# Loading the first scale group in two blocks on the ScalarE queue between exponentials, with c on the sync queue and a new k stage order

## The chip, the cores and the metric

The kernel runs on one core of a Trainium2 chip. The metric is the device time in microseconds (us) of one execution. The span of a profiled execution, from its first to its last instruction, is about 2 us shorter than the device time of the same execution (95.7 us of span for 97.58 us).

## The reference

It is the attention half of a diffusion transformer block with adaptive layer norm, in bfloat16, for B = 2, N = 256, D = 1152.

```
mod = silu(c) @ w_mod                      # c is B x D, w_mod is D x 6D
shift, scale, gate = three slices of mod
h = layernorm(x) * (1 + scale) + shift     # x is B x N x D
q, k, v = split(h @ wqkv)
a = (softmax(q @ k.T * D**-0.5) @ v) @ wo
return x + gate * a
```

## The kernel before

Tokens are four tiles of 128 (t = 0 to 3), features are nine slices of 128 (k = 0 to 8). A tile of x is normalised by VectorE, transposed by TensorE, multiplied by (1 + scale), and taken as the right operand of the k projection, feature slice by feature slice (`k_step(k, ...)`, weights `wK[k]`). The scale of a slice needs silu(c) and the matching part of the scale weights: nine small matmuls per slice. Those weights come in four groups, of 2, 2, 2 and 3 slices. The projection therefore can't start before x0 (tile 0 of x) is normalised and the first scale group has landed.

```python
load_x(syn, 0)                                    # sync queue
sca.dma_start(out=c_sb, in_=...)                  # c: ScalarE queue
S_GROUPS = SCALE_GROUPS                           # ((0, 2), (2, 4), (4, 6), (6, 9))
def load_scale(gi): ... syn.dma_start(out=wS_all[:, cols], in_=src)
...
junk(2)                                           # dummy 128x512 matmuls
ten.transpose(cT_ps, c_sb, ...)
sca.activation(out=e_sb, in_=cT_ps, func=ACT.Exp, scale=-1.0)
sca.activation(out=e_sb, in_=e_sb, func=ACT.Ln, bias=1.0)
sca.activation(out=e_sb, in_=e_sb, func=ACT.Exp, scale=-1.0)
...
junk(10)
stat_chunk(0, 1); stat_chunk(0, 0)
load_x(syn, 1); stat_sum(1); load_x(syn, 2)
...                                               # cut
norm(0, 0, 2); transposes(0, 0)
load_scale(0); scale_mods(0, 0, 9)                # first group: 576 KB, 18 small matmuls
...                                               # cut
load_wK(0); transposes(0, 1); load_wK(1)
k_step(0, 0, P); transposes(1, 0); ...; k_step(1, 0, P)
load_x(syn, 3); ...
load_scale(1); scale_mods(1, 0, 9)
...
```

Loads and their users are on different engines, so a load is issued as early as its own queue allows: the first scale group, behind the first transposes in the program, was issued at 2.11 us, before x0 had landed (3.61). On the sync queue the order is x0, x1, x2, first scale group, wK0, wK1, x3, second scale group, wK2, third scale group, and so on. Every load counts up one of eight completion semaphores, which are taken again in turn: the issue of a load waits until an earlier load on the same semaphore has landed. In the trace of this kernel the landings count on eight semaphores; the fourth scale group was issued at 8.40 us, after wK0 had landed at 8.39, and the load of wK behind it at 9.15, after wK1 had landed at 9.13.

## Time and profile before

| | before |
|---|---|
| device time, median (4 runs) | 98.44 us (98.36 to 98.59) |
| span of the profiled execution | 95.7 us |
| c landed | 2.85 us |
| x0, x1, x2 landed | 3.61, 4.36, 5.60 us |
| first scale group: issued, landed, first used | 2.11, 7.65, 7.91 us |
| wK0, wK1, second scale group landed | 8.39, 9.13, 11.32 us |
| first k step of slice 2 (`k_step(2, ...)`) starts | 12.72 us |

A landing here is the last increment of the load's completion semaphore in the trace, read to about 0.01 us; all times count from the start of the span.

The chain of waits, followed back from the last instruction (start us, us, what):

```profile
by line: PE ps L70 67.4%; PE acc_t L70 19.3%; PE psS L70 2.7%; DMA c_sb<-in_c_dram 2.2%; PE psH L70 2.2%; PE tp_t L70 1.7%; ACT o_sb L70 0.3%; DVE hTs L70 0.3%; PE cT_ps L70 0.2%; DVE s1p L70 0.2%; issue 0.2%; ACT L104 0.0%
...
0.75 2.10 DMA c_sb<-in_c_dram
...
3.52 4.38 PE acc_t L70 x10
...
8.11 0.49 PE psS L70 x18
...
12.38 0.30 DVE hTs L70
12.68 0.04 issue
12.72 1.14 PE acc_t L70 x9
```

In such lines PE is TensorE, DVE VectorE and ACT ScalarE; SPq and ACTq are issues on the sync and the ScalarE queue. psS is the result of the scale matmuls, tp_t of the transposes, acc_t of the dummies and the k steps; xn is a normalised tile, hTs a scaled one.

TensorE is the bound: after the load of c it runs nearly without a gap to the end. The ten dummies (3.52 to 7.9) keep it busy while the loads arrive. The waits of TensorE (in total, times, longest us) say the same: two, both before 3 us.

```profile
PE acc_t L70 <- DVE ones_w L70: 1.4, 1, 1.4
PE cT_ps L70 <- DMA c_sb<-in_c_dram: 0.4, 1, 0.4
```

### The profile page before, as it was taken

Reading aid. Unit: us, or ns where it says so; the run is one execution under the profiler, and the core shown is the slowest. Engines: PE = TensorE matmul, PEld = TensorE weight load, DVE = VectorE, ACT = ScalarE, POOL = GpSimd, SP = SyncE. Lnnn points to the kernel's source line nnn. Section 1 sums busy time; section 2 is a strip of 40 time slices with the busy share of each in tenths; the row PEclk is TensorE's granted clock in tenths of the full one; section 3 lists DMA queues with packets and bytes.
Section 4 is the critical chain, followed back from the end, with each engine's and each line's share of the span. In section 5 each row is a group of like instructions: output and inputs, shape, how many; then the busy total and the mean of one; then the engine's idle time right before and its main releaser. Section 6 shows DMA issues by size and latency. Waiting matters only on the chain.

```text
span 95.7 us, 1886 instructions
## 1 busy us (share of the span) xinstructions
PE 91.0 (95%) x771; PEld 60.9 (64%) x771; DVE 64.1 (67%) x131; ACT 32.3 (34%) x75; POOL 15.7 (16%) x11
## 2 busy tenths in 40 slices
PE   3899999999999999999999999999999999999980
PEld 0237989988899644444458765565568766556570
DVE  2487887050552999999999939910009599998780
ACT  5496988020421900003950084342335400000010
POOL 3020000000000000000000000079999900010000
PEclk9999999999999999999999999999999999999999
DMA  1999999999999999999993001122000000303122
GB/s 23 366 337 414 402 397 398 400 420 403 416 416 419 414 413 419 422 422 416 419 400 159 0 0 55 45 65 54 8 0 0 0 0 0 123 7 123 75 100 72
DMA packets 7379, 21.59 MB, mean 225 GB/s; under 512 B 2123, under 2 KB 2891, under 8 KB 7371
## 3 DMA queue, kind: packets, MB, share of 16 engines
q1 hardware_dynamic: 7200, 21.42, 57.7%
q8 instruction: 6, 0.10, 0.4%
q10 hardware_dynamic: 171, 0.05, 0.2%
q14 instruction: 2, 0.02, 0.0%
HBM read 19.76 MB, written 1.44 MB: 221 GB/s over the span
## 4 chain that ended last, share of the span: by engine, by line
PE 93%; DMA 2%; DVE 0%; ACT 0%; issue 0%
PE ps L70 67%; PE acc_t L70 19%; PE psS L70 3%; DMA c_sb<-in_c_dram 2%; PE psH L70 2%; PE tp_t L70 2%; ACT o_sb L70 0%; DVE hTs L70 0%; PE cT_ps L70 0%; DVE s1p L70 0%; ACT L104 0%
## 5 line engine op out<-in xcount | busy, mean ns | idle before, releaser
L70 POOL PARTITION_ALL_REDUCE gate_bc<-gacc x2 | 13.7, 6887 | 56.8 <-DVE gacc L70 56.8
L70 DVE SCALAR_TENSOR_TENSOR gacc<-wg_all,scT_f,gacc 128x1152 f32<-128x1152 bf16 x16 | 22.4, 1416 | 0.4
L70 PE MATMUL ps<-wV,hT 128*128 128x384 bf16 x108 | 17.7, 326 | 0.0
L70 PE MATMUL ps<-hT,wQ 128*128 128x512 bf16 x81 | 17.7, 379 | 0.0
L70 PEld LDWEIGHTS <-wK 128*128 128x128 bf16 x180 | 16.1, 98 | 1.8 <-issue 0.2
L70 PE MATMUL ps<-rows_t,attnT 128*128 128x384 bf16 (+3 forms) x108 | 17.0, 319 | 0.0
L70 PEld LDWEIGHTS <-attnT 128*128 128x128 bf16 x117 | 11.2, 98 | 6.4
L70 PEld LDWEIGHTS <-hT 128*128 128x128 bf16 x108 | 10.6, 98 | 6.9
L70 PE MATMUL acc_t<-hTs,wK 128*128 128x256 bf16 (+1 forms) x144 | 14.8, 259 | 0.1
L70 PEld LDWEIGHTS <-wQ 128*128 128x128 bf16 x81 | 7.9, 98 | 9.4
L70 ACT CAST v_sb<-ps 128x384 bf16<-128x384 f32 x12 | 5.8, 481 | 13.9 <-PE ps L70 13.9
L70 DVE CAST attnT<-ps 128x512 bf16<-128x512 f32 (+1 forms) x6 | 3.5, 603 | 9.5 <-PE ps L70 9.5
L70 ACT CAST qkT<-ps 128x512 bf16<-128x512 f32 x11 | 5.6, 610 | 12.6 <-PE ps L70 12.6
L70 DVE TENSOR_TENSOR ga<-ps,gate_bc 128x384 f32<-128x384 f32 (+3 forms) x12 | 6.4, 537 | 1.1 <-PE ps L70 1.0
L70 PE MATMUL acc_t<-ones_w 128*128 128x512 bf16 x12 | 5.5, 630 | 1.4 <-DVE ones_w L70 1.4
L70 DVE TENSOR_TENSOR o_sb<-ga,x_sb 128x384 bf16<-128x384 f32 (+3 forms) x12 | 6.5, 542 | 0.4
L70 ACT CAST o_sb<-ps 128x192 bf16<-128x192 f32 x1 | 0.3, 319 | 17.3 <-PE ps L70 17.3
L70 DVE CAST qkT<-acc_t 128x512 bf16<-128x512 f32 (+1 forms) x5 | 2.5, 576 | 4.5 <-PE acc_t L70 4.5
L70 DVE BATCH_NORM_STATS2 st_t<-x_sb 128x6 f32<-128x384 bf16 x6 | 3.1, 550 | 2.5 <-DMA x_sb<-in_x_dram 2.5
L70 PE MATMUL ps<-hTs,wK 128*128 128x256 bf16 x36 | 4.3, 272 | 0.0
L70 ACT ACTIVATE hTs<-xnT,s1p 128x128 bf16<-128x128 bf16 (+1 forms) x9 | 3.3, 417 | 2.8 <-DVE s1p L70 2.3
L70 PEld LDWEIGHTS <-ones_w 128*128 128x128 bf16 (+1 forms) x13 | 1.6, 135 | 4.1 <-issue 2.6
(59 smaller groups left out, 76.4 us busy)
## 6 DMA issues: line engine op xcount, KB each, us to landing
wK<-in_wk_dram SPq DMA_DIRECT2D x9, 288.0 KB, 8.3
rows_t<-in_w_shift_dram SPq DMA_DIRECT2D x3, 864.0 KB, 11.7
wQ<-in_wq_dram SPq DMA_DIRECT2D x3, 864.0 KB, 14.3
wg_all<-in_w_gate_dram SPq DMA_DIRECT2D x3, 864.0 KB, 14.4
wV<-in_wv_dram SPq DMA_DIRECT2D x3, 864.0 KB, 17.1
rows_t<-in_wo_dram SPq DMA_DIRECT2D x3, 864.0 KB, 17.1
wS_all<-in_w_scale_dram SPq DMA_DIRECT2D x3, 576.0 KB, 6.4
x_sb<-in_x_dram SPq DMA_DIRECT2D x4, 288.0 KB, 3.6
```

The source lines that it names most:

```text
L70: r = fn(*a, **k)
```

## The change

Its intent, as far as the code shows it: the first scale group is split, so that a first half can land sooner and on another queue than the x tiles; the sync queue is then free to ask for wK0 and wK1 earlier. One dummy goes, and the order of the k stage is redone to suit.

```diff
+    load_x(syn, 0)
+    syn.dma_start(out=c_sb, in_=...)
     nc.scalar.preload_act_table_set("natural_log_exp_and_others")
-    load_x(syn, 0)
-    sca.dma_start(out=c_sb, in_=...)
...
+    def load_block(j):                 # one slice, 288 KB
+        sca.dma_start(out=wS_all[:, cols], in_=w_scale[...])
...
     sca.activation(out=e_sb, in_=cT_ps, func=ACT.Exp, scale=-1.0)
+    load_block(0)
     sca.activation(out=e_sb, in_=e_sb, func=ACT.Ln, bias=1.0)
     sca.activation(out=e_sb, in_=e_sb, func=ACT.Exp, scale=-1.0)
+    load_block(1)
...
-    junk(10)
+    junk(9)
...
     transposes(0, 0)
-    load_scale(0)
-    scale_mods(0, 0, 9)
+    block_mods(0)
+    block_mods(1)
     norm(0, 2, KT)
...                                     # order of the later k steps; the last scale
...                                     # group is used after 22 k matmuls, not 32
```

In the compiled order, the sync queue now holds x0, c, x1, x2, wK0, wK1, x3, second scale group, wK2, third scale group. The issue of block 0 waits on x0's semaphore, that of block 1 on x2's.

More of the change, by code (lines that the diff above doesn't have):

```diff
@@ L102, in load_x @@
         eng.dma_start(out=x_sb[:, t, :], in_=x_f[t * P : (t + 1) * P, :])
+    load_x(syn, 0)
+    syn.dma_start(out=c_sb, in_=c.rearrange("b (k p) -> (b k) p", p=P))
     nc.scalar.preload_act_table_set("natural_log_exp_and_others")
-    load_x(syn, 0)
-    sca.dma_start(out=c_sb, in_=c.rearrange("b (k p) -> (b k) p", p=P))
     wmpool = ctx.enter_context(tc.tile_pool(name="wmpool", bufs=1))
@@ L123 @@
     wS_all = wmpool.tile([P, KT * D], BF16, tag="wS")
-    S_GROUPS = SCALE_GROUPS
+    S_GROUPS = ((0, 2), (2, 4), (4, 6), (6, 9))
     wS = []
@@ L133, in load_scale @@
         syn.dma_start(out=wS_all[:, cols], in_=src)
+    def load_block(j):
+        cols = slice(KT * P * j, KT * P * (j + 1))
+        sca.dma_start(out=wS_all[:, cols], in_=w_scale[P * cols.start : P * cols.stop].rearrange("(p n) -> p n", p=P))
     def load_wK(k):
@@ L277, in scale_mods, with block_mods @@
                 )
+    def block_mods(j):
+        w_j = wS_all[:, KT * P * j : KT * P * (j + 1)].rearrange("p (kk n) -> p kk n", kk=KT)
+        for kk in range(KT):
+            ten.matmul(
+                psS[:, j, :], lhsT=w_j[:, kk, :], rhs=sc_rhs(kk),
+                start=False, stop=(kk == KT - 1), skip_group_check=True,
+            )
     def copy_s1p(gi):
@@ L305, in k_step_b1 @@
             )
-    junk(10)
+    junk(9)
+    stat_chunk(0, 2)
+    load_x(syn, 1)
+    stat_chunk(0, 0)
+    stat_sum(1)
     stat_chunk(0, 1)
-    stat_chunk(0, 0)
-    load_x(syn, 1)
-    stat_sum(1)
+    silu_c()
+    stat_aggr(0)
     load_x(syn, 2)
-    stat_chunk(0, 2)
-    stat_aggr(0)
-    silu_c()
-    stat_chunk(2, 2)
     stat_chunk(2, 1)
@@ L319 @@
     stat_exp(0)
+    stat_chunk(2, 2)
+    stat_sq(1)
+    stat_ln2(1)
     norm(0, 0, 2)
     transposes(0, 0)
-    load_scale(0)
-    scale_mods(0, 0, 9)
+    block_mods(0)
+    block_mods(1)
     norm(0, 2, KT)
+    transposes(0, 1)
     stat_chunk(2, 0)
+    scaled_tp(0, 0, vec)
     stat_aggr(2)
-    scaled_tp(0, 0, vec)
+    load_wK(0)
+    k_step(0, 0, P)
+    stat_exp(1)
+    norm(1, 0, 2)
     scaled_tp(0, 1, vec)
-    stat_sq(1)
-    stat_ln2(1)
-    stat_exp(1)
     copy_s1p(0)
-    norm(1, 0, 2)
-    load_wK(0)
-    transposes(0, 1)
+    norm(1, 2, KT)
+    evac_tp(0, 1, sca, 0, 7)
+    transposes(1, 0)
+    scaled_tp(1, 1, vec)
+    scaled_tp(1, 0, vec)
     load_wK(1)
-    norm(1, 2, KT)
+    k_step(1, 0, P)
     stat_ln(2)
-    k_step(0, 0, P)
-    transposes(1, 0)
-    scaled_tp(1, 0, vec)
-    evac_tp(0, 1, sca, 0, 7)
-    k_step(1, 0, P)
-    load_x(syn, 3)
     transposes(1, 1)
-    k_step(0, P, N)
-    scaled_tp(1, 1, vec)
-    k_step(1, P, N)
     stat_exp(2)
     norm(2, 0, 2)
+    k_step(0, P, N)
+    load_x(syn, 3)
+    stat_sum(3)
+    k_step(1, P, N)
+    norm(2, 2, KT)
     evac_tp(1, 1, vec, 0, 7)
-    norm(2, 2, KT)
+    stat_sq(3)
+    stat_ln2(3)
     load_scale(1)
@@ L359 @@
     evac_tp(2, 1, vec, 0, 7)
-    stat_sum(3)
-    stat_sq(3)
-    stat_ln2(3)
     stat_exp(3)
@@ L367 @@
     norm(3, 2, KT)
+    scaled(3, 0, vec)
     evac_tp(2, 0, sca, 0, 2)
-    scaled_t(0, 2, vec)
     transposes(3, 0)
     load_scale(2)
-    scaled_t(3, 2, vec)
-    scaled(3, 0, sca)
+    scale_mods(2, 0, 9)
     evac_tp(3, 0, sca, 0, 2)
     scaled_t(0, 3, sca)
-    scale_mods(2, 0, 9)
-    copy_s1p(2)
-    scaled_t(5, 2, vec)
-    scaled_t(2, 2, sca)
     transposes(3, 1)
+    evac_tp(3, 1, vec, 0, 7)
+    scaled_t(1, 2, vec)
     load_wK(3)
     k_step(3, 0, N)
-    evac_tp(3, 1, vec, 0, 7)
+    copy_s1p(2)
+    scaled_t(5, 3, vec)
+    scaled_t(3, 3, vec)
+    scaled(5, 0, vec)
+    scaled_t(1, 3, sca)
+    scaled_t(0, 2, sca)
     alloc_b1()
+    k_step_b1(0, [0])
+    scaled_t(3, 2, sca)
     k_step_b1(0, [1, 2, 3, 4])
-    scaled_t(1, 2, vec)
-    scaled_t(3, 3, vec)
-    load_wK(5)
-    scaled(5, 0, vec)
-    k_step_b1(0, [0])
-    scaled_t(5, 3, sca)
-    k_step(5, 0, N)
+    k_step_b1(1, [1, 2, 3, 4])
+    scaled_t(5, 2, sca)
+    scaled(4, 0, vec)
     k_step_b1(3, [1, 2, 3, 4])
-    scaled_t(1, 3, vec)
+    scaled_t(2, 2, vec)
+    load_scale(3)
+    scale_mods(3, 0, 9)
+    scaled_t(4, 3, vec)
     scaled_t(4, 2, sca)
     scaled_t(2, 3, sca)
-    k_step_b1(2, [1, 2, 3, 4])
-    load_scale(3)
-    k_step_b1(5, [0])
-    scale_mods(3, 0, 9)
-    scaled_t(4, 3, vec)
-    scaled(4, 0, sca)
     copy_s1p(3)
-    scaled(6, 0, vec)
+    scaled(6, 0, sca)
     scaled_t(6, 2, vec)
@@ L407 @@
     scaled(7, 0, vec)
-    scaled_t(7, 2, vec)
+    scaled_t(7, 2, sca)
     scaled_t(7, 3, vec)
     scaled(8, 0, vec)
-    scaled_t(8, 2, sca)
+    scaled_t(8, 2, vec)
     scaled_t(8, 3, sca)
     load_wK(4)
+    load_wK(5)
     load_wK(6)
@@ L418 @@
     k_step_b1(1, [0])
-    k_step_b1(1, [1, 2, 3, 4])
     k_step_b1(2, [0])
+    k_step_b1(2, [1, 2, 3, 4])
     k_step_b1(3, [0])
@@ L424 @@
     k_step_b1(4, [1, 2, 3, 4])
+    k_step(5, 0, N)
+    k_step_b1(5, [0])
     k_step_b1(5, [1, 2, 3, 4])
@@ L669 @@
         pin(rec.seq)
-SCALE_GROUPS = ((0, 2), (2, 4), (4, 6), (6, 9))
+SCALE_BLOCKS = ((0, 1), (1, 2), (2, 4), (4, 6), (6, 9))
 _OUTS = [((2, 256, 1152), 'bfloat16')]
@@ L690, in _packed @@
     scale = rows(w_mod[:, D : 2 * D]).transpose(1, 0, 2)
-    scale = _np.concatenate([scale[:, :, k0 * P : k1 * P].reshape(-1) for k0, k1 in SCALE_GROUPS])
+    scale = _np.concatenate([scale[:, :, k0 * P : k1 * P].reshape(-1) for k0, k1 in SCALE_BLOCKS])
     return {
```

## The prediction

> **What bounds the kernel now.** TensorE. In the chain of waits it holds 93% of the 95.7 us span, in an unbroken run: the chain has 2.1 us of load of c (0.75 to 2.85 us), then the c transpose, 0.43 us of psS initialisation, ten dummy 512-column matmuls (4.38 us at the slow clock, 0.43 us each), and from 7.9 us real work with one gap, about 0.5 us at 12.2 us (scale copy, one hTs operation). So the time is: start of the real work + a fixed sum of TensorE work + idle.
>
> The front is also close to what the loads give. By issue plus time to landing: x0 lands at 3.6, x1 4.4, x2 5.6, the first scale group (576 KB) at 7.65, wK0 at 8.4, wK1 at 9.1, the second scale group at 11.3. TensorE starts on the first scale group at 7.8 and on the second at 11.5: a margin of 0.2 us each.
>
> **What the change does.** TensorE's list differs in order, and in one dummy less: -0.43 us if nothing else holds it.
>
> Added or moved:
> 1. c goes behind x0 on one queue. x0's packets end at 3.1 us, its landing is 3.6; c should land at about 3.5 instead of 2.85. The c transpose starts 0.65 us later, so nine dummies end near 7.9: the removed dummy is about paid back (net +0.2).
> 2. ScalarE now issues two loads; one issue costs 0.33 to 0.45 us on SyncE (0.59 for c on ScalarE's queue), estimated 0.45 each. The second also waits on x2's semaphore (seen in the instruction order), so ScalarE is held until about 5.5. Then the sum over x1 (1.16), ln and exp: rstd of tile 0 at about 7.6 instead of 6.05, so the first norm gives its tile to TensorE near 8.0 instead of 7.3. The dummies hide that no longer.
> 3. Block 0 (288 KB) is issued at about 4.1 and block 1 near 5.6. [...] Sharing a measured 340 to 410 GB/s in half, a block needs some 1.5 us: block 0 lands near 7.2, block 1 near 8.6. Block 1 stalls TensorE perhaps 0.2 us.
> 4. ScalarE's square pass over x1 ends near 9.2 (before 7.3), so norm(1) comes at 9.6 instead of 9.1: 0 to 0.5 us stall before the transposes of tile 1.
> 5. Against this: the later order (22 instead of 32 k matmuls before the last scale group, that group loaded one wK earlier) only moves work in a stage without idle: about 0. The gap at 12.2 may shrink.
>
> Sum: -0.4 +0.65 +0.3 (stalls) -0.4 (gap, and the chance that c lands sooner): about +0.1 us.
>
> **Prediction:** 98.6 us, 8 in 10 within 97.7 to 99.7. Faster by over 2%: 0.04; within 2%: 0.90; slower by over 2%: 0.06.
>
> **To check in the profile:** c's landing (3.5); the first transposes of xn (7.9 to 8.2); a wait of psS matmuls on the block loads; rstd of tile 0 near 7.6; TensorE idle between 8 and 13 us (0.5 to 1.2); nothing changed after 20 us but a shift.
>
> **What would make it wrong:** c landing at once with x0's first packets (gain 0.5); [...] blocks starved behind SyncE's deep queue (loss 1).

That two queues share the bandwidth in half was an assumption of mine; the windows of before show 341 to 417 GB/s from 5 to 11 us, and the 1.5 us and the two landings are estimates from that. The slow clock is seen in the trace of before: its ten dummies start 0.43 us apart, and the first clock record is one of full clock, from 8.03 us; later, from 32.2 us on, 512-column matmuls come every 0.22 us (60 in 13.13 us).

## More of the kernel before

The timeline of the first stage, cut to the lines of the argument (start us, us, engine, line, operation):

```profile
2.11 0.43 SPq L70 DMA_DIRECT2D wS_all<-in_w_scale_dram  x1
...
7.91 0.69 PE L70 MATMUL psS<-scT_rep,wS_all 128*128 128x56 bf16 x18
...
8.44 0.55 PE L70 MATMUL tp_t<-ident,xn 128*128 128x128 bf16 x7
8.64 0.48 DVE L70 TENSOR_SCALAR hTs<-tp_t,psS 128x128 bf16<-128x128 bf16 x2 [0.59 <-PE psS L70]
```

The group issued at 2.11 us is used at 7.91 us, 0.26 us after it landed. So the front is bound by TensorE and by the loads at once: a first scale group that lands more than this 0.26 us later stops TensorE directly.

## The result and the profile after

| | before | after |
|---|---|---|
| device time, median (4 runs each) | 98.44 us | 105.72 us (104.96 to 105.97) |
| ratio, 95% interval | | 1.0725 (1.0664 to 1.0785) |
| span | 95.7 us | 103.2 us |
| c landed | 2.85 | 3.36 |
| rstd of tile 0 (1 over its standard deviation, from ScalarE) done | 6.05 | 8.54 |
| x0, x1, x2 landed | 3.61, 4.36, 5.60 | 3.65, 5.24, 6.46 |
| scale weights of slice 0 / slice 1: issued | 2.11 (one load) | 3.67 / 6.48 |
| the same: landed | 7.65 | 10.71 / 13.43 |
| transposes behind the scale matmuls start | 8.44 | 13.89 |
| first k step of slice 2 starts | 12.72 | 20.03 |

Ratios are the mean time of one kernel's fast runs over that of the other's in the same rounds, so they aren't quite the ratio of the medians.

The waits of TensorE after:

```profile
PE psS L70 <- DMA wS_all<-in_w_scale_dram: 3.8, 2, 2.3
PE acc_t L70 <- DVE ones_w L70: 1.4, 1, 1.4
PE tp_t L70 <- DVE xn L70: 1.0, 1, 1.0
PE cT_ps L70 <- DMA c_sb<-in_c_dram: 0.9, 1, 0.9
```

Two lines are new. The first, 3.8 us, is TensorE waiting for each of the two blocks. The timeline of the changed kernel, with the issues on the ScalarE queue and their users:

```profile
3.67 0.37 ACTq L70 DMA_DIRECT2D wS_all<-in_w_scale_dram  x1
...
6.48 0.34 ACTq L70 DMA_DIRECT2D wS_all<-in_w_scale_dram  x1
...
6.86 1.16 ACT L70 ACTIVATE scr<-x_sb 128x1152 f32<-128x1152 bf16 x1 [2.31 <-DMA x_sb<-in_x_dram]
...
8.34 0.20 ACT L70 ACTIVATE rstd<-lnv 128x1 f32<-128x1 f32 x1
...
8.98 0.28 PE L70 MATMUL tp_t<-ident,xn 128*128 128x128 bf16 x2 [1.00 <-DVE xn L70]
...
10.76 0.41 PE L70 MATMUL psS<-scT_rep,wS_all 128*128 128x56 bf16 x9 [1.50 <-DMA wS_all<-in_w_scale_dram]
13.47 0.60 PE L70 MATMUL psS<-scT_rep,wS_all 128*128 128x56 bf16 x9 [2.31 <-DMA wS_all<-in_w_scale_dram]
...
13.89 0.93 PE L70 MATMUL tp_t<-ident,xn 128*128 128x128 bf16 x7
```

Block 0 took 7.0 us from issue to landing, block 1 6.9 us. The second issue also held ScalarE from 4.6 to 6.48 us, until x2 had landed, which is why rstd of tile 0 came 2.5 us later and TensorE waited 1.0 us for xn.

The last line differs in its duration as well: seven transposes took 0.55 us before and 0.93 us here. The windows of the two kernels show why. Columns: stretch, its length, busy us of each engine (instructions), granted clock, DMA share, GB/s. Before:

```profile
14.00:16.00 2.00, 2.00 (x38) 1.87 (x34) 1.80 (x9) 1.54 (x5) 0.00 (x0) 1.00 1.03 413
```

After:

```profile
10.00:12.00 2.00, 0.41 (x9) 0.29 (x9) 0.00 (x0) 0.31 (x2) 0.00 (x0) 0.84 1.04 397
12.00:14.00 2.00, 0.53 (x11) 0.53 (x12) 0.00 (x0) 0.00 (x0) 0.00 (x0) 0.50 1.06 423
14.00:16.00 2.00, 2.00 (x22) 2.00 (x20) 1.31 (x6) 1.11 (x3) 0.00 (x0) 0.50 1.00 408
16.00:18.00 2.00, 2.00 (x21) 2.00 (x20) 1.41 (x5) 1.97 (x4) 0.00 (x0) 0.50 1.04 393
```

TensorE, idle for most of 9 to 13.5 us (busy for 0.67 us of it), was put on half clock from 11.34 to 18.17 us and ran its next 4.7 us of work at that. The DMA was busy throughout (around 400 GB/s): it carried other loads.

The sum closes. The transposes behind the scale matmuls start 5.45 us later (13.89 - 8.44). The stage from there to the k step of slice 2 takes 6.14 us (20.03 - 13.89) instead of 4.28 (12.72 - 8.44), 1.86 us more. Together that is 7.31 us, of 7.41 us of span (103.16 - 95.75). From the k step of slice 2 to the first shift matmul both kernels take 15.42 us.

One view misleads here. The chain of waits of the changed kernel:

```profile
4.38 8.60 DMA wK<-in_wk_dram
12.97 0.02 issue
12.99 7.05 DMA wK<-in_wk_dram
20.04 1.13 PE acc_t L70 x9
```

It puts the delay on loads of wK. The x9 group at 20.04 is the k step of slice 2. It needs wK2, which landed at 12.97, and the scaled tile, which VectorE wrote from 19.69 to 19.98. The load that the chain names was issued at 12.99 and holds another slice: it only landed at nearly the same moment. In the chain of before, the same group is released by VectorE's hTs.

### The profile page after: what moved, and what is told of

Same layout as the page of the kernel before. It is cut to its first block, busy times and chain, and to the rows that moved or that the text cites. A ratio compares the mean times of both kernels' runs of the same rounds, so it can differ in the third digit from the quotient of the medians.

```text
span 103.2 us, 1884 instructions
## 1 busy us (share of the span) xinstructions
PE 92.9 (90%) x768; PEld 62.7 (61%) x770; DVE 63.9 (62%) x130; ACT 32.6 (32%) x76; POOL 15.8 (15%) x11
## 4 chain that ended last, share of the span: by engine, by line
PE 78%; DMA 15%; SPq 3%; issue 1%; ACT 0%
PE ps L70 62%; DMA wK<-in_wk_dram 15%; PE acc_t L70 12%; SPq L70 3%; PE psH L70 2%; PE psS L70 1%; PE tp_t L70 0%; ACT o_sb L70 0%
## 5 line engine op out<-in xcount | busy, mean ns | idle before, releaser
L70 PEld LDWEIGHTS <-wK 128*128 128x128 bf16 x180 | 17.3, 105 | 1.7 <-issue 0.2
L70 PE MATMUL acc_t<-hTs,wK 128*128 128x256 bf16 (+1 forms) x144 | 16.1, 275 | 0.1
L70 PE MATMUL psS<-scT_rep,wS_all 128*128 128x56 bf16 x81 | 3.1, 192 | 3.8 <-DMA wS_all<-in_w_scale_dram 3.8
L70 PEld LDWEIGHTS <-wS_all 128*128 128x128 bf16 x81 | 2.7, 99 | 4.1 <-DMA wS_all<-in_w_scale_dram 4.1
L70 PE MATMUL tp_t<-ident,xn 128*128 128x128 bf16 x36 | 4.1, 261 | 1.0 <-DVE xn L70 1.0
```

The lines of the kernel that those rows point to most:

```text
L70: r = fn(*a, **k)
```

## The experiments

Theories at the outset: the blocks land late ("queue theory"; later split into place in line against a slow second queue); the later c spoils the start; the new order costs; the half clock adds. Ten edited kernels ran, and the changed kernel once more, all with correct results. Each edited one was timed in three rounds beside the kernel before, whose medians in the three sessions were 98.47, 98.21 and 98.40 us. An execution is labelled slow when it lies over 1.5% above the fastest of the same kernel.

### a_c_sync

```diff
 # kernel before
-    sca.dma_start(out=c_sb, in_=...)
+    syn.dma_start(out=c_sb, in_=...)
```

> The kernel before with one edit: c goes on the sync queue behind x0. Queue theory (the loss is the late landing of the two scale blocks on the ScalarE queue): the first scale group stays on the sync queue, lands at about 7.7 us, so the time is within 0.6 us of before (98.4 to 99.1). Rival, the c theory (the later c, 3.40 instead of 2.85 us, breaks the start and the clock's warm-up): 100 us or more, with a granted clock or TensorE gaps like the changed kernel's.

Measured: 98.51 us, ratio 1.0027 (0.998 to 1.0075). c landed at 3.68 us and the first scale group at 8.32. Moving c isn't the cause: with its interval it is worth 0.75% at the most.

### b_blocks_sync

```diff
 # changed kernel
-    load_block(0)    # between the exponentials, ScalarE queue
-    load_block(1)
     load_x(syn, 2)
+    load_block(0)    # sync queue, ahead of wK0
+    load_block(1)
```

> The changed kernel with one edit: the two blocks are issued on the sync queue behind x2, before wK0 (nine dummies, c on sync, new k order all kept). Queue theory: blocks land at about 6.9 and 7.7 us, time 97.9 to 99.2. Order theory (the new k stage order costs the time): stays at 103 or more.

Measured: 99.09 us, ratio 1.0076 (1.0016 to 1.0136). The blocks landed at 7.26 and 8.68 us (expected 6.9 and 7.7). With everything else of the change kept, nine tenths of the loss are gone (0.8% instead of 7.3%). This edit changes the queue, the moment of issue and the place in line at once, so it can't tell them apart.

### c_act_blocks

```diff
 # kernel before
     sca.activation(out=e_sb, in_=cT_ps, func=ACT.Exp, scale=-1.0)
+    load_block(0)
     ...
     sca.activation(out=e_sb, in_=e_sb, func=ACT.Exp, scale=-1.0)
+    load_block(1)
-    load_scale(0); scale_mods(0, 0, 9)
+    block_mods(0); block_mods(1)
```

> The kernel before with only the first scale group changed to two blocks on the ScalarE queue between the exponentials (c, dummies and k order as before). Queue theory: blocks land near 10.5 and 13 us and the time is 103.5 to 106.5. Order or c theory: within 1 us of before.

Measured: 104.39 us, ratio 1.0629 (1.0581 to 1.0677). The blocks landed at 11.20 and 13.25 us, and TensorE waited 4.5 us for them; it was on half clock for 6.83 us here too. The two block loads alone bring most of the loss.

### d_act_early

```diff
 # changed kernel
+    load_block(0)    # ScalarE queue, ahead of the first exponential
+    load_block(1)
     sca.activation(out=e_sb, in_=cT_ps, func=ACT.Exp, scale=-1.0)
-    load_block(0)
     ...
-    load_block(1)
```

> The changed kernel with the two block issues moved ahead of the exponentials, so that ScalarE issues them at about 0.8 us, still on its own queue. If the loss is late issue (3.67 and 6.48 us, the second held by the wait on x2): blocks land by 5 to 6 us, time 98 to 99.5, x0 lands later than 3.65. If the ScalarE queue itself is starved beside the sync queue whenever both have work: blocks still land after 9 us and the time is 102 or more.

Measured: median 99.71 us over all four runs; ratio 1.0074 (1.002 to 1.0127). The issues:

```profile
0.75 0.87 ACTq L70 DMA_DIRECT2D wS_all<-in_w_scale_dram  x2
```

The blocks landed at 4.68 and 5.34 us, on the same queue that had taken until 10.71 and 13.43. So the ScalarE queue isn't slow in itself. x0 (4.51) and c (4.90) came later for it, and TensorE waited 2.5 us for c. The transposes behind the scale matmuls then started at 10.39 us (8.44 before), still at the slow clock, which rose at 11.33 us here (8.03 before). That this is all that remains of the time isn't shown.

### e_hold

```diff
 # changed kernel
     load_x(syn, 2)
+    hold = dram.tile([1, 2 * KT], F32, tag="hold")
+    syn.dma_start(out=hold, in_=e_sb[0:1, :])
```

> The changed kernel, with one small store of one row of e_sb put on the sync queue behind x2: it waits for the exponentials (about 4.6 us), so wK0, wK1, x3 and the later loads are issued after block 0 instead of before it. The blocks stay on the ScalarE queue between the exponentials. Place-in-line theory (a load moves only when the bytes issued before it, on either queue, have moved): block 0, issued near 3.7 us, has its first packet by 5.5 and lands by 6.8; block 1 by 8.2; time 98.5 to 100.5, the loads after them about 0.7 us later. Second-queue theory (the ScalarE queue is served slowly whatever was issued before): block 0 lands after 9, time over 102.

Measured: 100.05 us, ratio 1.0222 (1.0135 to 1.0308). Block 0 was issued at 3.83, had its first packet at 4.92 and landed at 7.49 us (expected: by 6.8); block 1 landed at 8.21. The issues, with that of the small store (`hold`) and of wK0 and wK1 behind it:

```profile
3.83 0.37 ACTq L70 DMA_DIRECT2D wS_all<-in_w_scale_dram  x1
4.50 0.34 ACTq L70 DMA_DIRECT2D wS_all<-in_w_scale_dram  x1
4.73 0.25 SPq L70 DMA_DIRECT2D hold<-e_sb  x1
5.02 0.80 SPq L70 DMA_DIRECT2D wK<-in_wk_dram  x2
```

TensorE's waits were now short ones on the whole line of loads:

```profile
PE psS L70 <- DMA wS_all<-in_w_scale_dram: 1.4, 3, 0.8
PE cT_ps L70 <- DMA c_sb<-in_c_dram: 1.1, 1, 1.1
PE acc_t L70 <- DMA wK<-in_wk_dram: 0.8, 1, 0.8
```

For block 0 it is the same queue and nearly the same moment of issue: only the loads issued ahead on the other queue were fewer. It landed 3.2 us sooner. For block 1 the run is less clean, since it was also issued 2 us sooner (4.50 instead of 6.48). And 2.2% of loss stay, with an interval from 1.35 to 3.1%.

### f_sync_late2

A first build, f_sync_late, in program order put the loads of the blocks behind the matmuls that read them, so uninitialised memory was read. The mended one:

```diff
 # changed kernel; both blocks on the sync queue, loads taken out at their old places
     load_x(syn, 2)
+    load_wK(0); load_wK(1); load_x(syn, 3)
+    load_block(0)
+    load_scale(1); load_wK(2); load_scale(2)
+    load_block(1)
```

> The changed kernel with both blocks on the sync queue, but at the places in the line of issues that they have in the changed kernel: block 0 behind x3, block 1 behind the third scale group. Place-in-line theory: block 0 lands at 8.3 to 9.5, block 1 at 12.0 to 14.0, time 103 to 106.5, close to the changed kernel though no second queue is used. Second-queue theory (most of the delay is the sharing between two queues): block 1 lands before 10.5, time under 101.5.

Measured: 105.78 us over six runs, ratio 1.0754 (1.0676 to 1.0832). The profile fell in an execution labelled slow (106.87 us), so only its shape is used: block 0 landed at 10.30 and block 1 at 14.70 us.

```profile
PE psS L70 <- DMA wS_all<-in_w_scale_dram: 6.1, 2, 3.8
```

Without a second queue, but with the same place in the line of issues, the loss is as large as the changed kernel's. Both blocks came later than expected (8.3 to 9.5 and 12.0 to 14.0), in an execution that was itself slow. ScalarE, which issued no block here, had rstd of tile 0 done at 6.79 us, not 8.54, and that saved nothing. So neither a second queue nor ScalarE's delay is needed for the loss. With d_act_early and e_hold, where the second queue was quick, this decides for place in line against a slow second queue.

### g_warm

```diff
 # changed kernel
+    junk(8)
     block_mods(0)
+    junk(11)
     block_mods(1)
```

> The changed kernel with 8 dummies before the first block's matmuls and 11 before the second's, into TensorE's waits, so that its clock does not fall to half. If the half clock from 11.3 to 18.2 us adds to the loss: 0.9 to 1.9 us faster than the changed kernel, 103.6 to 104.8. If the stage after the blocks is bound by loads or VectorE, no change: 105.0 to 106.0. If the waits were the whole loss and the dummies overrun them: over 106.

Measured: 103.31 us in the profiled execution and 102.79 us in the fast timed one; two more timed ones, 104.94 and 105.43, are labelled slow. The ratio of fast runs, 1.0506 (1.0408 to 1.0605), rests on few runs. The windows of the profiled execution, and two lines of its timeline:

```profile
12.00:14.00 2.00, 2.00 (x20) 1.06 (x19) 0.00 (x0) 0.00 (x0) 0.00 (x0) 1.00 1.03 414
14.00:16.00 2.00, 2.00 (x38) 1.89 (x35) 1.83 (x9) 1.48 (x4) 0.00 (x0) 1.00 1.02 417
...
13.90 0.55 PE L70 MATMUL tp_t<-ident,xn 128*128 128x128 bf16 x7
...
18.19 1.14 PE L70 MATMUL acc_t<-hTs,wK 128*128 128x256 bf16 x9
```

The stage from the transposes (13.90) to the k step of slice 2 (18.19) takes 4.29 us: that of before was 4.28, that of the changed kernel 6.14. The dummies overran block 1 (landed at 12.60, used at 13.67), so the transposes start when they do in the changed kernel (13.89) and the comparison is clean: the half clock costs 1.85 us there. The span fell from 103.2 to 101.5 us. The two fast executions lie a little below the range that I gave (103.6 to 104.8).

### h_order_only

```diff
 # changed kernel
-    load_block(0); load_block(1)    # between the exponentials
-    block_mods(0); block_mods(1)
+    scale_mods(0, 0, 9)      # one load_scale(0) on sync behind x2
-    junk(9)
+    junk(10)
 # c back on the ScalarE queue
```

> The new k stage order alone: loads of the first scale group and of c, and ten dummies, as in the kernel before. If the new order is neutral: 98.0 to 98.9. If the new order itself is worth something (fewer k matmuls before the last scale group): 97.0 to 98.0; if it costs: over 99.

Measured: 98.76 us, ratio 1.0071 (1.0009 to 1.0133). The order is worth nothing and costs a little. Its profile has two waits of TensorE that before has not: 0.57 us for the first normalised tile (x2 landed at 7.20 us in this execution), and this one for the last scale group, at 18.56 us:

```profile
18.56 0.87 PE L70 MATMUL psS<-scT_rep,wS_all 128*128 128x56 bf16 x27 [0.39 <-DMA wS_all<-in_w_scale_dram]
```

With 22 k matmuls instead of 32 ahead of it, TensorE gets there before the load does. How the 0.7% divides between the two isn't shown.

### k_pair

```diff
 # changed kernel
     load_block(0)
+    load_block(1)
     sca.activation(out=e_sb, in_=e_sb, func=ACT.Ln, bias=1.0)
     sca.activation(out=e_sb, in_=e_sb, func=ACT.Exp, scale=-1.0)
-    load_block(1)
```

> The changed kernel with block 1 issued directly behind block 0 on the ScalarE queue. By the instruction order it then waits on x1's landing (about 5.2 us) instead of x2's (6.46). Place-in-line theory: the 576 KB of the third scale group are no longer ahead of it, so block 1 lands at 11.3 to 12.4 us instead of 13.4, block 0 still at 10 to 11; the time falls by 1 to 2 us, to 103.7 to 104.8. If block 1's landing is set by something else (for instance block 0 and block 1 following each other on one queue): no change, 105 or more.

Measured: 103.68 us, ratio 1.0539 (1.0471 to 1.0607). Block 1 was issued at 5.87 us, when x1 had landed, ahead of the third scale group (6.60), and landed at 12.65 (expected 11.3 to 12.4); block 0 at 10.67. The step is in the direction and near the size expected. The time gained more than block 1's 0.8 us: the half clock lasted 3.41 us here (12.18 to 15.60), not 6.83.

### i_early_act

```diff
 # kernel before
     sca.dma_start(out=c_sb, in_=...)
+    load_block(0)
+    load_block(1)
-    junk(10)
+    junk(9)
-    load_scale(0); scale_mods(0, 0, 9)
+    block_mods(0); block_mods(1)
```

> The kernel before with the first scale group as two blocks on the ScalarE queue directly behind c, before anything else there, and nine dummies: the change's intent with an early place in the line. Place-in-line theory: blocks land at 5 to 6.8 us, x0 by 4.2, time 97.6 to 98.9, so within 1% of before, because the second scale group (11.3 us) still sets the next stage. If a second queue costs by itself: over 99.5.

Measured: 97.75 us in the profiled execution and 99.01 us in the one timed execution that is labelled fast; the two others, 100.04 and 99.98, are labelled slow. The ratio on record, 1.0144 (1.0066 to 1.0222), is near what all three timed runs give, slow ones included, and its verdict is unclear. In the profile the blocks landed at 5.18 and 7.89 us, x0 at 3.65, and TensorE waited 0.3 us for them. No starvation, and no gain that these runs can show: of the two fast executions one lies in the range that I gave and one 0.1 us above it. Why the four spread by more than 2 us is open. No version that I built is shown to beat the kernel before.

### after_again

> The changed kernel once more, for a second trace of the clock: place-in-line and clock theory expect block 0 at 10 to 11.5 us and block 1 at 13 to 14 us, half clock in the wait or a clock that never rose before it, time 104.5 to 106.5.

Measured: 104.61 us (state unknown, a single run). The blocks landed at 11.32 and 13.90 us. Its mean granted clock:

```profile
core 0: 102.8 us, clock 0.997
```

One window of the same trace, and a line of its timeline:

```profile
14.00:16.00 2.00, 2.00 (x25) 2.00 (x26) 1.31 (x6) 0.67 (x1) 0.00 (x0) 1.00 1.06 431
...
14.36 0.93 PE L70 MATMUL tp_t<-ident,xn 128*128 128x128 bf16 x7
```

The column says full clock, yet TensorE does only 25 matmuls in these 2 us, near the 22 of the first trace at half clock and far from the 38 of g_warm in the same stretch. The clock records of this execution begin at 16.92 us with the rise to full clock; what lies ahead of the first record counts as full. TensorE was slow up to there: seven transposes at 14.36 us took 0.93 us, as in the first trace. This is how an execution of the changed kernel can show a clock of 1.0 and be no faster, as two of the four timed ones did (105.97 and 105.93 us); that it was so in those two, of which there is no trace, is an inference.

### The place in line, in six runs

First packets are read from the packet records of the traces (on the sync queue by counting 128 packets to a 288 KB load in the order of issue). The count is only good to a few tenths of a us by my estimate: in f_sync_late2 it puts block 0's first packet at 8.26 us, 0.13 us behind that of the second scale group, which was issued after it on the same queue.

| run | block 0: issued, first packet, landed | block 1: issued, first packet, landed | issued ahead of block 0 |
|---|---|---|---|
| changed kernel | 3.67, 6.75, 10.71 | 6.48, 10.08, 13.43 | x0, c, x1, x2, wK0, wK1, x3 |
| f_sync_late2 (one queue) | 3.90, 8.26, 10.30 | 6.72, 11.99, 14.70 | the same |
| k_pair | 3.74, 7.09, 10.67 | 5.87, 9.74, 12.65 | the same |
| e_hold | 3.83, 4.92, 7.49 | 4.50, 6.30, 8.21 | x0, c, x1, x2 |
| i_early_act | 1.38, 3.61, 5.18 | 1.78, 5.09, 7.89 | x0, c, x1 |
| d_act_early | 0.75, 1.97, 4.68 | 1.17, 3.92, 5.34 | x0 |

In these six runs, on whichever queue, a block started when nearly all that was issued ahead of it had started. In the changed kernel, x3 was issued at 3.43, block 0 at 3.67 and the second scale group at 3.90 us; their first packets came at 7.01, 6.75 and 7.64 us. Four loads of 288 KB issued ahead of block 0 had yet to start at 3.67, and block 0 began when three of them had begun. Then it took 3.3 us, while x3 and most of the 576 KB of the second scale group moved too; in e_hold, with little beside it, it took 1.8 us. The order is no strict one: block 0 started 0.26 us ahead of x3, and block 1 (10.08) 0.58 us ahead of the third scale group (10.66), which had been issued 1.22 us earlier. c_act_blocks and after_again, not in the table, look alike: block 0 issued at 4.41 and 3.86, first packets at 8.14 and 7.31 us.

## Why the prediction was wrong

The measured 105.72 us lies far outside 97.7 to 99.7. The frame was right: start of the real work, plus a fixed sum of TensorE work, plus idle; the later stages only shifted. Point by point:

- **c behind x0: right.** Predicted 3.5 us, 3.36 measured; the nine dummies ended at 7.98 (predicted 7.9). In a_c_sync the move costs nothing that can be told from zero.
- **The failed step is 3, where the prediction says "Sharing a measured 340 to 410 GB/s in half, a block needs some 1.5 us: block 0 lands near 7.2, block 1 near 8.6".** Measured: 10.71 and 13.43. The issues were not far off (3.67 and 6.48 us for 4.1 and 5.6); from issue to landing the prediction has some 3 us for each block, and the runs show 7.0 and 6.9. TensorE waited 3.8 us for the blocks, not "perhaps 0.2". I took the ScalarE queue to have half the bandwidth from about 1 us after the issue, an assumption. d_act_early comes near it where two loads are issued at the same time: x0 and block 0, issued at 0.73 and 0.75 us, moved side by side (1.74 to 3.94 and 1.97 to 3.92 us). But with a backlog, in the changed kernel, the block began 3.1 us after its issue (3.67 to 6.75 us, behind seven issued loads), not 1.2 (0.75 to 1.97 in d_act_early, behind one), in the line of what had been issued before, on either queue. f_sync_late2 shows that the second queue is not needed for the loss, e_hold that without the backlog most of it goes (2.2% instead of 7.3%). That a load is taken up in the order of issue, give or take one load, is what all six rows of the table fit; why the hardware does so, none of the runs shows.
- **ScalarE's delay (step 2) was mis-sized.** The wait on x2 was foreseen, until 5.5 us; x2 landed at 6.46. From 3 to 7 us the changed kernel's DMA moved 270 to 313 GB/s, before's 274 to 406. So rstd of tile 0 came at 8.54 instead of 7.6, TensorE's first transposes at 8.98 instead of 8.0. It was hidden behind the blocks, and so was a stall for tile 1 (step 4). Why the DMA was slower there is open: a_c_sync and b_blocks_sync, which also have c behind x0, show 235 to 359 and 187 to 295 GB/s, but d_act_early, which has it too, 325 to 414.
- **A missing term: the clock.** The forecast has no term for a clock that falls again during a wait. In the changed kernel the clock was full from 7.93 us, half from 11.34 to 18.17 (6.83 us) and full again; in k_pair it was half for 3.41 us, from 12.18 to 15.60. In the 3.41 us ahead of the fall, TensorE's instructions fill 0.74 us in the changed kernel and 0.65 us in k_pair. In g_warm, with dummies in the waits, TensorE was busy for 11.57 of the 12 us from 8 to 20 us, its windows show full clock, and its seven transposes took 0.55 us (0.93 in the changed kernel). How much work would have kept the clock isn't shown. The half clock cost 1.86 us of 7.3, and g_warm gave back 1.85 us of the stage.
- **The new order (step 5): "about 0".** h_order_only measured 0.7% (interval 0.1 to 1.3%), in part through an early arrival at the last scale group.
- **The list of dangers held the cause, as "blocks starved behind SyncE's deep queue (loss 1)".** That is what the runs come nearest to, but the size was wrong: TensorE's waits for the blocks alone were 3.8 us. A better estimate could have been made from the trace of before: the loads issued near 4 us there landed 6.4 to 7.4 us later (x3: issued 3.53, landed 9.88; wK2: 4.72, 12.07). By these times, a load issued at 3.67 us would be estimated to land near 10 to 11.

So the gain that was intended went as follows: the first half of the scale group was asked for 1.6 us later than the whole had been (3.67 against 2.11 us), behind three loads (wK0, wK1, x3) that are used after it; the second half was asked for 4.4 us later, held by a semaphore wait. TensorE stood still for both, and went to half clock in the second stand; with dummies in both stands, in g_warm, it did not.

## What to carry to other kernels

In these runs a load began when the loads issued before it, on both queues together, had begun, to within about one load; and it landed later still when others moved beside it (block 0 took 3.3 us once begun in the changed kernel, 1.8 in e_hold). The second queue didn't let a late load pass the backlog (block 0 landed at 10.71 us on its own queue, at 10.30 on the common one). So order the issues by need over all queues, and cost a moved load with the issue-to-landing time that the old profile shows at that moment (6.4 to 7.4 us here; the block then took 7.0, against 3.7 in e_hold and 3.9 in d_act_early), not with the bandwidth. A stall of some microseconds on TensorE (3.8 us here) can also have a second price, work at half clock afterwards (1.86 us here): look at matmul durations for it, not only at the mean clock.
